# Attention with a gated convolution FFN on one core: low parts of the weights by TensorE and ScalarE, later q and k of the first batch transposed by TensorE, its V loaded for the whole batch, and order and banks from fixed tables

## The chip, the cores and the metric

The kernel runs on one core of a Trainium2 chip. The metric is the device time of one execution in microseconds (us). PE is TensorE, DVE VectorE, ACT ScalarE, POOL GpSimd; SP issues most DMAs. PEld is the loading of the stationary operand, which overlaps PE.

## The reference

```
scores = (q @ k.T) / 8, masked so that block i of 64 positions sees blocks j <= i
attn = softmax(scores);  x = attn @ v, heads put side by side     # [8, 576, 512]
h = relu(x @ w_in)                                                # [8, 576, 1024]
c[s] = w0*h[s-1] + w1*h[s] + w2*h[s+1]                            # per feature
out = (h * sigmoid(c)) @ w_out                                    # [8, 576, 512]
```

There are 8 batches, 8 heads of width 64, 576 positions, all in float32. The weights `w_in`, `conv_w` and `w_out` arrive as 64-bit floats and are turned into 32-bit ones on the chip ("decode").

## The kernel before, in words

**Arithmetic.** The two large products run in a short float format (float32r) that TensorE takes in one pass. To keep the precision, each operand is split into a high part, its float32r rounding, and a low part, the rest. A product is three matmuls: high by high, high by low, low by high. The parts are `wih`, `wil` for `w_in`, `woh`, `wol` for `w_out`, `x` (two halves) for the attention output and `gh`, `gl` for the gated hidden values. Scores and the product with V run in plain float32, in tiles of 64 rows by 32 columns.

**Attention.** Heads go in pairs, four pairs to a batch, 32 visits in all; the first batch is cut in two parts, so that its work can begin before the weights are there: part A takes the first 256 positions of four pairs, part B the other 320. A visit is: q and k transposed (by PE in part A, line 960; by DVE from a 32-by-32 layout otherwise, line 981, with q scaled by POOL on line 975), score matmuls (line 1010), row maxima on DVE (1023), exponentials with sums on ACT (1028), a merge of statistics (1044 to 1065), the scaling of the probabilities on POOL (1077), their transposition on DVE (1096), the product with V (1109), and the split of its result: ACT writes the high part (1123), DVE subtracts it from the PSUM bank and writes the low part (1126).

**FFN.** The batch is cut into two runs of positions ("halves"). Per half there are 8 chunks of 128 features. Twelve matmuls make a chunk (line 1156); ACT and DVE apply relu, convolution and gate (1170 to 1193), ACT writes `gh` (1193), POOL subtracts and writes `gl` (1196). The second layer takes, per 128 positions, three matmuls for each chunk (line 1222); ACT evicts and SP stores the result.

**Weights.** Sixteen chunks (eight of `w_in`, the first in two pieces, eight of `w_out`) are decoded by ACT (774), POOL (780) and DVE (785 to 808), POOL adding two parts on line 812 for four of them. ACT makes the high part (843). For twelve chunks the low part goes through PE: minus the high part (859) plus the decoded low term (862) is summed in a bank, and DVE adds the decoded main term to it (865). For four chunks POOL subtracts (846).

**Order.** Nothing is scheduled by hand. Every operation is recorded in a plan with a target time from a table of numbers (`TARGETS`). `Plan.order` then plays the engines forward with assumed durations, picks for each engine the ready operation with the least target, and hands out the eight PSUM banks as it goes. Where it expects PE to wait over 0.4 us, it puts in **fillers**: matmuls of a constant that nobody reads (line 1317), 512 columns each, 173 in all. Each engine executes its list in order.

Of the kernel before, what the change touches and what calls it, by code (L numbers as in the profile page):

```python
# [11 lines left out]
F32 = mybir.dt.float32  # L12
# [8 lines left out]
TARGETS = """  # L21
# [237 lines left out]

class Plan:  # L260

    DRAIN = (0.165, 0.08, 0.1, 0.025, 0.0)
    SIGNAL = (0.04, 0.035, 0.035, 0.08, 0.1)

    def __init__(self):
        self.ops = []
        self.tags = {}  # L270
        self.queue = {}

    def bank(self, slots, tag):
        b = Bank(slots, tag)
        q = self.queue.setdefault(tag, [])
        b.index = len(q)
        q.append(b)
# [36 lines left out]
    def order(self, targets, skip, fill, clock, pair):  # L314
# [13 lines left out]
        def use(o):  # L328
            t = o.start
            while t < o.end:  # L330
                w = int(t / step)
                u = min(o.end, (w + 1) * step)
                if u <= t:
                    u = t + 1e-6
# [1019 lines left out]
```

## Time and profile before

| | us |
|---|---|
| median of 3 runs | 749.32 (747.5 to 750.0) |
| the profiled execution | 750.95 |
| its span, first to last instruction | 749.2 |
| busy: PE, DVE, ACT, POOL | 687.9, 588.6, 528.2, 447.2 |

The profiled execution is 1.6 us above the median, and 1.75 us of it lie outside the span. PE's busy time counts fillers too, and records of neighbouring matmuls overlap, so that a busy PE need not be one at full rate.

### The profile page before, as it was taken

How to read it: one execution, taken by the hardware profiler on the slowest of the kernel's cores; microseconds unless marked ns; L12 is line 12 of the kernel's file. 1: busy time of each engine (PE TensorE's matmuls, PEld its weight loads, DVE VectorE, ACT ScalarE, POOL GpSimd, SP SyncE). 2: the span in 40 equal slices, each digit the busy share in tenths (PEclk: the TensorE clock that was granted, in tenths of full speed). 3: DMA queues.
4: the chain of work that ended last, by engine and by line, in shares of the span. 5: the costliest groups of instructions: out<-in, count | busy, mean ns of one | idle time of the engine just before them, and what ended most of it. 6: DMA issues, size and time to landing. Idle time of an engine off the chain costs nothing.

```text
span 749.2 us, 29948 instructions
## 1 busy us (share of the span) xinstructions
PE 687.9 (92%) x12112; PEld 562.6 (75%) x12112; DVE 588.6 (79%) x1422; ACT 528.2 (71%) x1987; POOL 447.2 (60%) x926
## 2 busy tenths in 40 slices
PE   8889887999989999898989989998989999998998
PEld 6567757767868787776868777786878687787986
DVE  5799996997888877898869868878868969876543
ACT  6667655787777757786877668767678768794554
POOL 1555884887467752767565746657546754776232
PEclk9999998999999999999999999999999999999999
DMA  8853655137423342335422352344304362122001
GB/s 197 179 108 74 125 124 110 32 71 150 82 44 85 67 106 34 77 70 90 83 64 46 54 130 50 57 93 81 74 12 90 79 126 35 44 52 63 1 29 43
DMA packets 238671, 58.59 MB, mean 78 GB/s; under 512 B 228652, under 2 KB 233028, under 8 KB 238532
## 3 DMA queue, kind: packets, MB, share of 16 engines
q1 hardware_dynamic: 237988, 56.55, 37.2%
q8 instruction: 95, 1.56, 0.9%
q14 instruction: 44, 0.36, 0.2%
q10 hardware_dynamic: 544, 0.13, 0.1%
HBM read 47.21 MB, written 9.44 MB: 76 GB/s over the span
## 4 chain that ended last, share of the span: by engine, by line
DVE 34%; ACT 18%; PE 17%; POOL 13%; issue 7%; DMA 5%; SPq 4%; DVEq 0%; POOLq 0%; ACTq 0%
ACT p L1028 11%; POOL p L1077 10%; DVE st L1023 7%; DVE ptw L1096 6%; PE banks L1222 6%; PE banks L1156 5%; DVE t L1177 4%; PE banks L1109 4%; DVE t L1181 4%; DVE t L1189 3%; PE banks L1010 2%; POOL gl L1196 2%; DMA kn<-in_k_dram 2%; ACT t L1173 2%; SPq L721 2%
## 5 line engine op out<-in xcount | busy, mean ns | idle before, releaser
L1077 POOL TENSOR_SCALAR p<-p,st 128x160 f32<-128x160 f32 (+8 forms) x576 | 247.7, 448 | 84.4 <-DVE st L1065 80.8
L1028 ACT ACTIVATE p<-banks,st 128x32 f32<-128x32 f32 (+8 forms) x576 | 220.4, 401 | 61.8 <-DVE st L1023 42.2
L1156 PE MATMUL banks<-x,wih 128*128 128x290 f32 (+3 forms) x1024 | 191.1, 302 | 4.2 <-DVE x L1126 1.7
L1196 POOL TENSOR_TENSOR gl<-t,gh 128x289 fp32r<-128x289 f32 (+3 forms) x128 | 108.2, 854 | 113.8 <-ACT gh L1193 99.3
L1156 PEld LDWEIGHTS banks<-x,wih 128*128 128x128 f32 x1024 | 156.1, 189 | 17.8 <-issue 4.2
L1096 DVE STREAM_TRANSPOSE ptw<-p 128x448 f32<-128x448 f32 (+8 forms) x272 | 131.6, 504 | 38.7 <-POOL p L1077 34.9
L1023 DVE TENSOR_REDUCE st<-banks 128x2 f32<-128x192 f32 (+8 forms) x288 | 127.3, 471 | 6.3 <-PE banks L1010 5.6
L1222 PE MATMUL banks<-woh,gl 128*128 128x512 f32 (+1 forms) x296 | 117.9, 398 | 7.7 <-POOL gl L1196 7.2
L1028 ACT ACTIVATION_READ_ACCUMULATOR p<-banks,st 128x1 f32 x576 | 122.8, 213 | 0.0
L1222 PE MATMUL banks<-woh,gh 128*128 128x512 f32 (+1 forms) x296 | 119.6, 404 | 1.1 <-ACT h L1170 0.6
L1222 PE MATMUL banks<-wol,gh 128*128 128x512 f32 (+1 forms) x296 | 115.7, 391 | 0.8 <-POOL wol L846 0.8
L1109 PE MATMUL banks<-ptw,vn 64*32 64x160 f32 (+8 forms) x4608 | 94.9, 300 | 22.1 <-issue 9.7
L1010 PE MATMUL banks<-kT,qT 64*32 64x96 f32 (+8 forms) x4320 | 100.7, 303 | 14.3 <-ACT p L1028 7.7
L1109 PEld LDWEIGHTS banks<-ptw,vn 64*32 64x32 f32 x4608 | 82.1, 107 | 39.9 <-issue 13.9
L1156 PE MATMUL banks<-x,wil 128*128 128x290 f32 (+3 forms) x512 | 108.8, 299 | 0.0
L1010 PEld LDWEIGHTS banks<-kT,qT 64*32 64x32 f32 x4320 | 66.7, 105 | 43.0 <-ACT p L1028 14.2
L1177 DVE SCALAR_TENSOR_TENSOR t<-h,cw,t 128x289 f32<-128x289 f32 (+3 forms) x128 | 70.4, 559 | 30.4 <-ACT t L1173 30.2
L1156 PEld LDWEIGHTS banks<-x,wil 128*128 128x128 f32 x512 | 82.8, 190 | 2.1 <-issue 1.3
L1186 ACT ACTIVATE t<-t 128x287 f32<-128x287 f32 (+3 forms) x128 | 56.4, 446 | 30.8 <-DVE t L1181 30.0
L1222 PEld LDWEIGHTS banks<-woh,gl 128*128 128x128 f32 x296 | 55.8, 189 | 28.7 <-POOL gl L1196 17.0
L1181 DVE SCALAR_TENSOR_TENSOR t<-h,cw,t 128x288 f32<-128x288 f32 (+3 forms) x128 | 73.0, 579 | 1.0
L1189 DVE SCALAR_TENSOR_TENSOR t<-t,h 128x287 f32<-128x287 f32 (+3 forms) x128 | 64.7, 511 | 10.0 <-ACT t L1186 9.6
(91 smaller groups left out, 801.6 us busy)
## 6 DMA issues: line engine op xcount, KB each, us to landing
vn<-in_v_dram SPq DMA_DIRECT2D x128, 144.0 KB, 3.7
out_dram<-stage SPq DMA_DIRECT2D x35, 256.0 KB, 2.6
kn<-in_k_dram SPq DMA_DIRECT2D x112, 72.0 KB, 2.7
qn<-in_q_dram SPq DMA_DIRECT2D x112, 72.0 KB, 2.5
x<-in_moe_w_out_dram SPq DMA_DIRECT2D x8, 512.0 KB, 4.5
gl<-in_moe_w_in_dram SPq DMA_DIRECT2D x4, 512.0 KB, 5.5
gh<-in_moe_w_in_dram SPq DMA_DIRECT2D x3, 512.0 KB, 5.3
vxa<-in_v_dram SPq DMA_DIRECT2D x16, 64.0 KB, 4.1
```

The lines of the kernel that those rows point to most:

```text
L1010: nc.tensor.matmul(both(sb)[32 * quad:32 * quad + 32, h, o:o + w].rearrange("p (u n) -> p u n", n=32), t["q"].ap[r, 64 * b + 32 * g:64 * b ...
L1023: nc.vector.tensor_reduce(out=st.ap[:, c:c + 2], in_=both(sb)[:, :, off:off + w], op=ALU.max, axis=AX.X, negate=True)
L1028: nc.scalar.activation(out=pt.ap[:, h, :], in_=both(sb)[:, h, off:off + w], func=AF.Exp, bias=st.ap[:, c:c + 1], accum_out=st.ap[:, n + c: ...
L1077: nc.gpsimd.tensor_scalar(out=pt.ap[:, h, :], in0=pt.ap[:, h, :], scalar1=st.ap[:, 5 * n + c:5 * n + c + 1], scalar2=0.0, op0=ALU.mult, op ...
L1096: nc.vector.transpose(pt.ap[:, :, b:b + rise * b + 1:rise, :], x.ap.rearrange("p h (u n) -> p h u n", n=32))
L1109: nc.tensor.matmul(both(vb)[o:o + 32, g, 32 * (lo - b0):32 * (b1 - b0)].rearrange("p (b n) -> p b n", n=32), vat(u, h)[r, 32 * y:32 * y + ...
L1156: nc.tensor.matmul(fb.ap[:, 0:n2], wt[:, c, fs], xs[c][xi].ap[:, x0:x0 + n2], start=(n + c - c0 == 0), stop=(n + c - c0 == 3 * NCC - 1))
L1177: nc.vector.scalar_tensor_tensor(out=t.ap[:, i0:no], in0=hb.ap[:, own + i0 - 1:own + no - 1], scalar=cw[:, f:f + 1], in1=t.ap[:, i0:no], o ...
L1181: nc.vector.scalar_tensor_tensor(out=t.ap[:, 0:i1], in0=hb.ap[:, own + 1:own + 1 + i1], scalar=cw[:, 2 * NFC + f:2 * NFC + f + 1], in1=t.a ...
L1189: nc.vector.scalar_tensor_tensor(out=t.ap[:, 0:no], in0=t.ap[:, 0:no], scalar=1.0, in1=hb.ap[:, own:own + no], op0=ALU.add, op1=ALU.mult)
L1196: nc.gpsimd.tensor_tensor(out=gbuf[1].ap[:, f, carry:carry + no], in0=t.ap[:, 0:no], in1=gbuf[0].ap[:, f, carry:carry + no], op=ALU.subtract)
L1222: nc.tensor.matmul(fb.ap[:, 0:cut], gbuf[a].ap[:, f, cs], w[:, f, ds], start=(f == 0 and n == 0), stop=(f == NFC - 1 and n == 2))
```

## The change

All 16 weight chunks now get their low part through PE and ACT. A third matmul brings the decoded main term into the same bank, in plain float32 against the identity, and ACT writes the sum out as the low part; the subtraction on DVE and that on POOL are gone, and so is the sum on POOL. The same is done for the low part of the attention output in the first batch: PE subtracts the high part in the bank, and ACT writes what is left. In part B, q and k come in rows of 64 values, PE transposes them (three matmuls for each of q and k of a pair) and ACT evicts them, scaling q. The values of V that part A needs are loaded by eight DMAs of 64 rows of all heads, instead of sixteen by head, and each product with V in part A waits for all eight. Two of the first weight loads are issued by ACT instead of SP. `Plan.order` is replaced by `Plan.follow`, which emits the operations in the order of a list, with the banks of a second list and 100 fillers at the places of a third.

```diff
@@ Plan
-    def order(self, targets, skip, fill, clock, pair):
...
+    def follow(self, order, banks, fills, work):
...
+        for x in order:
+            o = self.ops[x]
+            if x in fills:
+                z, k = fills[x]
...
+                work(z, k)()
...
+            o.fn()
@@ load_b (new; part B)
+                    nc.sync.dma_start(out=n.ap[0][0:r, c], in_=src[0, h0:h0 + 2, s:s + r, :].rearrange("h p d -> p h d"))
@@ load_first
-                        nc.sync.dma_start(out=vxa[64 * y:64 * y + 64, 2 * g + j],
-                                          in_=v[0, 2 * g + j, 0:Q1, :].rearrange("(u p) d -> p u d", p=64))
...
+                    nc.sync.dma_start(out=vxa[64 * y:64 * y + 64, :, u, :],
+                                      in_=v[0, :, 64 * u:64 * u + 64, :].rearrange("h p d -> p h d"))
@@ split
-        def fl():
-            nc.gpsimd.tensor_tensor(out=lo, in0=src(), in1=hi, op=ALU.subtract)
...
+        def mid():
+            nc.tensor.matmul(fb.ap[:, 0:n_], ident, scratch(None), start=False, stop=False)
...
         def fl2():
-            nc.vector.tensor_tensor(out=lo, in0=view(), in1=src(), op=ALU.add)
+            nc.scalar.activation(out=lo, in_=view(), func=AF.Copy)
@@ load_w_in
+            queue = nc.scalar if 0 < f + h < 2 else nc.sync
@@ later_t (new; part B)
+                    nc.tensor.matmul(tb.ap[:, c * P:c * P + r].bitcast(F32R), n.ap[1][0:r, c].rearrange("p j d -> p (j d)"), rident[0:r, 0:r],
+                                     start=(c == 0), stop=True, is_transpose=True, skip_group_check=True)
...
+            es.append(copy_op(False, S - Q1, lambda hi=hi: hi.ap[:, Q1:], lambda tb=tb: tb.ap[:, 0:S - Q1], at + 0.3, [o], [tb, hi], scale))
@@ stage_pv
+                nc.tensor.matmul(got()[:, g], nident, dst(0)[:, g], start=False, stop=True, skip_group_check=True)
...
+            nc.scalar.activation(out=dst(1), in_=got(), func=AF.Copy)
@@ end
-    for o in pl.order([int(x) for x in TARGETS.split()], SKIP, (work, psum, (NBANK0, NBANK, TB), 0.234, LEAST, SPARE), CLOCK, (NEAR, FAR, BIAS)):
-        o.fn()
+    pl.follow(ORDER, BANKS, FILLS, lambda z, k: work(psum[z], k))
```

What moves on the engines is seen in three places. In the lists below a row is a line of the kernel, an operation, what it writes and reads, and its size; the changed kernel's lines have other numbers.

**DVE, the first weight chunks.** `gh` is the staging buffer of a chunk here. Before:

```order
L801 TENSOR_SCALAR gh<-gh 128x256
L808 SCALAR_TENSOR_TENSOR wil<-gh 128x2x128
L865 TENSOR_TENSOR wil<-banks,gh 128x2x128
L785 TENSOR_SCALAR gh<-gh 128x512
L797 SCALAR_TENSOR_TENSOR gh<-gh 128x512
L801 TENSOR_SCALAR gh<-gh 128x512
L808 SCALAR_TENSOR_TENSOR wil<-gh 128x4x128
L1023 TENSOR_REDUCE st_277<-banks 128x2 x4
L865 TENSOR_TENSOR wil<-banks,gh 128x4x128
```

and now:

```order
L618 SCALAR_TENSOR_TENSOR gh<-gh 128x256
L622 TENSOR_SCALAR gh<-gh 128x256
L876 TENSOR_REDUCE st_267<-banks 128x2 x2
L632 SCALAR_TENSOR_TENSOR wil<-gh 128x2x128
L876 TENSOR_REDUCE st_267<-banks 128x2 x2
L904 TENSOR_TENSOR st_194<-st_194 128x8
L632 SCALAR_TENSOR_TENSOR wil<-gh 128x4x128
```

The final sum from the bank (L865) has left DVE in each chunk; the other steps stay.

**PE, ahead of the second product with V in part B.** `kX` and `kT` are transposed k, `ptw` the transposed probabilities, `vn` V, `rident` the constant of the fillers. Before:

```order
L1010 MATMUL banks<-kX,qT 32x160 x8
L1317 MATMUL banks<-rident 128x512 x41
L1109 MATMUL banks<-ptw,vn 32x160 x40
L1109 MATMUL banks<-ptw,vn 32x128 x8
L1109 MATMUL banks<-ptw,vn 32x96 x8
```

and now:

```order
L863 MATMUL banks<-kX,qT 32x288 x8
L863 MATMUL banks<-kX,qT 32x192 x8
L1020 MATMUL banks<-x,wih 128x256 x2
L814 MATMUL banks<-rident,kn_97 128x128 x2
L814 MATMUL banks<-rident,kn_97 128x64
L1020 MATMUL banks<-x,wil 128x256 x2
L1020 MATMUL banks<-x,wih 128x256 x2
L1181 MATMUL banks<-rident 128x512 x8
L962 MATMUL banks<-ptw,vn 32x160 x40
```

Of 41 fillers 8 are left; first-layer matmuls (L1020) and transposes (L814) stand between the scores and the product. Counted over the list up to the end of the fourth such product, fillers fall from 171 to 86, first-layer matmuls stay at 108, and second-layer ones go from 18 to 21.

**POOL, the fourth batch, chunks five and six of its first half.** The scalings of the probabilities (L1077, now L930) and the low parts `gl` (L1196, now L1060) share POOL's list. Before:

```order
L975 TENSOR_SCALAR qn<-qn 128x576
L1077 TENSOR_SCALAR p_6271<-p_6271,st_6226 128x64 x2
L1077 TENSOR_SCALAR p_6278<-p_6278,st_6226 128x128 x2
L1077 TENSOR_SCALAR p_6295<-p_6295,st_6226 128x32
L1077 TENSOR_SCALAR p_6285<-p_6285,st_6226 128x96
L1077 TENSOR_SCALAR p_71<-p_71,st_6226 128x160 x2
L1077 TENSOR_SCALAR p_6285<-p_6285,st_6226 128x96
L1196 TENSOR_TENSOR gl<-t,gh 128x287 x2
```

and now:

```order
L930 TENSOR_SCALAR p_71<-p_71,st_6148 128x160 x2
L930 TENSOR_SCALAR p_6191<-p_6191,st_6148 128x128 x2
L930 TENSOR_SCALAR p_6180<-p_6180,st_6148 128x32
L930 TENSOR_SCALAR p_6230<-p_6230,st_6148 128x64
L930 TENSOR_SCALAR p_6180<-p_6180,st_6148 128x32
L930 TENSOR_SCALAR p_6230<-p_6230,st_6148 128x64
L1060 TENSOR_TENSOR gl<-t,gh 128x287
L930 TENSOR_SCALAR p_6225<-p_6225,st_6148 128x96 x2
L505 TENSOR_SCALAR st_6337<-st_6337 32x16
L1060 TENSOR_TENSOR gl<-t,gh 128x287
```

Nine scalings stood ahead of the two low parts; now eight stand ahead of the first one. Over the 112 low parts behind the first batch, those with eight or more scalings right ahead of them go from 10 to 7.

## Rows read from the trace of the kernel before

**Rows 1.** The page, part 1: busy us of each engine (share of the span)

```profile
PE 687.9 (92%) x12112; PEld 562.6 (75%) x12112; DVE 588.6 (79%) x1422; ACT 528.2 (71%) x1987; POOL 447.2 (60%) x926
```

**Rows 2.** Stretches: busy of PE, PEld, DVE, ACT, POOL; clock, DMA share, GB/s

```profile
0.00:43.00 43.00, 35.69 (x560) 25.85 (x560) 29.09 (x86) 27.19 (x106) 17.88 (x47) 1.00 0.88 192
43.00:118.70 75.70, 67.09 (x1319) 51.25 (x1317) 72.95 (x173) 51.19 (x186) 51.36 (x92) 1.00 0.51 103
118.70:128.20 9.50, 6.34 (x35) 5.76 (x34) 4.39 (x11) 3.14 (x15) 5.68 (x11) 0.64 0.60 110
128.20:700.00 571.80, 532.93 (x9935) 439.57 (x9935) 458.21 (x1107) 418.72 (x1613) 356.67 (x758) 1.00 0.35 70
```

**Rows 3.** Waits of PE, 128.2 to 700 us: us, times, longest

```profile
PE banks L1222 <- POOL gl L1196: 7.2, 9, 1.5
```

**Rows 4.** POOL timeline, 366 to 382 us

```profile
375.28 3.98 POOL L1077 TENSOR_SCALAR p<-p,st 128x64 f32<-128x64 f32 x9 [0.73 <-DVE st L1065]
```

**Rows 5.** By stretch, of the fillers on line L1317 alone

```profile
0.00:43.00 43.00, 23.55 (x82) 15.90 (x82) 1.00 0.88 192
43.00:118.70 75.70, 23.02 (x91) 16.09 (x89) 1.00 0.51 103
```

**Rows 6.** PE timeline, 70 to 87 us: start, us, what, idle before

```profile
73.48 9.60 PE L1317 MATMUL banks<-rident 128*128 128x512 f32 x41
85.16 2.07 PE L1109 MATMUL banks<-ptw,vn 64*32 64x160 f32 x118 [2.07 <-ACT stage L774]
```

**Rows 7.** Chain of waits, first 45 us: start, us, what

```profile
36.45 6.56 DMA kn<-in_k_dram
```

**Rows 8.** PE timeline, 104 to 124 us

```profile
103.60 1.04 PE L1010 MATMUL banks<-kT,qT 64*32 64x288 f32 x32
...
116.55 2.18 PE L1109 MATMUL banks<-ptw,vn 64*32 64x160 f32 x131 [0.24 <-ACT st L1044]
121.89 0.35 PE L1109 MATMUL banks<-ptw,vn 64*32 64x32 f32 x13 [3.16 <-issue]
```

**Rows 9.** DVE groups, 0 to 128.2 us: count, busy us, mean ns

```profile
L1126 DVE TENSOR_TENSOR x<-banks,x 128x256 fp32r<-128x256 f32 (+1 forms) x8 | 3.5, 442 | 0.0
...
L865 DVE TENSOR_TENSOR wil<-banks,gh 128x512 fp32r<-128x512 f32 (+1 forms) x5 | 2.9, 574 | 0.9 <-PE banks L862 0.9
...
L865 DVE TENSOR_TENSOR wil<-banks,gl 128x512 fp32r<-128x512 f32 x4 | 2.7, 677 | 0.0
L865 DVE TENSOR_TENSOR wol<-banks,stage 128x512 fp32r<-128x512 f32 x4 | 2.7, 672 | 3.4 <-PE banks L862 3.4
```

**Rows 10.** DVE groups of the whole run, shapes apart

```profile
L981 DVE STREAM_TRANSPOSE qT<-qn 128x320 f32<-128x320 f32 x4 | 2.0, 504 | 0.7 <-POOL qn L975 0.7
...
L981 DVE STREAM_TRANSPOSE kT<-kn 128x320 f32<-128x320 f32 x2 | 1.0, 512 | 2.7 <-DMA kn<-in_k_dram 2.7
L981 DVE STREAM_TRANSPOSE kX<-kn 128x320 f32<-128x320 f32 x2 | 1.0, 508 | 0.0
```

**Rows 11.** Line L865 by stretch

```profile
43.00:118.70 75.70, 3.35 (x5) 1.00 0.51 103
```

**Rows 12.** Line L1126 by stretch

```profile
43.00:118.70 75.70, 2.26 (x5) 1.00 0.51 103
```

**Rows 13.** ACT groups, 0 to 128 us, shapes apart

```profile
L843 ACT ACTIVATE wih<-gl 128x512 fp32r<-128x512 f32 x4 | 2.6, 639 | 0.4 <-DVE gl L797 0.4
...
L1123 ACT ACTIVATE x<-banks 128x320 fp32r<-128x320 f32 x4 | 1.7, 434 | 2.3 <-PE banks L1109 2.3
```

**Rows 14.** POOL groups, 0 to 128 us, shapes apart

```profile
L812 POOL TENSOR_TENSOR stage<-stage,x 128x512 f32<-128x512 f32 x3 | 4.1, 1360 | 0.7 <-POOL st L696 0.7
...
L846 POOL TENSOR_TENSOR wol<-stage,woh 128x512 fp32r<-128x512 f32 x3 | 3.9, 1293 | 0.9 <-ACT woh L843 0.9
```

**Rows 15.** PE timeline, 22 to 25 us

```profile
22.93 0.60 PE L1109 MATMUL banks<-pta,vxa 64*32 64x128 f32 x26 [0.19 <-DVE pta L1096]
```

**Rows 16.** SP timeline, 26 to 45 us

```profile
27.73 1.26 SPq L762 DMA_DIRECT2D vxa<-in_v_dram  x2
```

More of the change, by code (lines that the diff above doesn't have):

```diff
@@ L1 @@
-import heapq
-from collections import deque
 from functools import partial
@@ new lines, in follow @@
+    def follow(self, order, banks, fills, work):
+        order = [int(x) for x in order.split()]
+        place = {x: i for i, x in enumerate(order)}
+        assert len(place) == len(order) == len(self.ops)
+        for o in self.ops:
+            assert all(place[d.seq] < place[o.seq] for d in o.deps)
+        every = [b for q in self.queue.values() for b in q]
+        banks = "".join(banks.split())
+        assert len(banks) == len(every)
+        for b, z in zip(every, banks):
+            b.slot, b.left = int(z), len(b.uses)
+        tenant = {}
+        fills = {int(x): (int(z), int(k)) for x, z, k in (f.split(":") for f in fills.split())}
+        for x in order:
+            o = self.ops[x]
+            if x in fills:
+                z, k = fills[x]
+                assert tenant.get(z) is None
+                work(z, k)()
@@ L504, in order @@
             for b in o.banks:
+                assert tenant.get(b.slot) in (None, b)
+                tenant[b.slot] = b
                 b.left -= 1
-                b.rel = max(b.rel, o.end + o.lat + self.DRAIN[e] + self.SIGNAL[PE] if e != PE else o.end)
                 if not b.left:
-                    tenant[b.slot], freed[b.slot], past[b.slot] = None, b.rel, b.uses
-                    gone[b.tag] += 1
-            free[e] = o.end
-            if o.port:
-                port = o.end
-            done.append(o)
@@ L514, in order @@
-            for c in o.outs:
-                c.left -= 1
-                lat = self.DRAIN[e] + (self.SIGNAL[c.eng] if c.eng != e else 0.0) if (e != PE or c.eng != PE) else 0.0
-                rtime[c.seq] = max(rtime[c.seq], o.end + o.lat + lat)
-                if e != PE:
-                    wtime[c.seq] = early[c.seq] = rtime[c.seq]
-                if c.left == 0:
-                    if c.eng == PE:
-                        open_.append(c)
-                    else:
-                        heapq.heappush(future[c.eng], (rtime[c.seq], c.target, c.seq, c))
@@ L525, in order @@
-        done.sort(key=lambda o: o.start)
-        return done
+                    tenant[b.slot] = None
+            o.fn()
 @with_exitstack
@@ L639 @@
     firstq, firstp = Bin([]), Bin([])
+    qkn = []
+    for x in "qk":
+        at = place(x + "n", S)
+        qkn.append([fixed(f"{x}n{y}", s, d, at) for y, (s, d) in enumerate((([P, S // 32, 32], F32), ([P, 3, 2, D], F32), ([P, 3, 2, D], F32R)))])
     def held(tag, t, cap, before=None):
@@ L724, in load_qk, with load_b, go @@
             res.append((n, ops))
+        return res
+    def load_b(p, at):
+        h0, res = 2 * p, []
+        for z, src in enumerate((q, k)):
+            n = held(("qn", "kn")[z], [qkn[z][1:]], 1)
+            def go(src=src, n=n):
+                for c in range(3):
+                    r = min(P, S - Q1 - c * P)
+                    s = Q1 + c * P
+                    nc.sync.dma_start(out=n.ap[0][0:r, c], in_=src[0, h0:h0 + 2, s:s + r, :].rearrange("h p d -> p h d"))
+            res.append((n, [pl.op(SP, 1.7, go, at + 0.1 * z, bufs=[n], xfer=c_dma(2 * (S - Q1) * D * 4, 256))]))
         return res
@@ L811, in s7, with s8 @@
             def s7(j=j, words=words):
-                nc.gpsimd.tensor_tensor(out=scratch(j), in0=scratch(j), in1=words(1).bitcast(F32), op=ALU.add)
+                ap = [words(0).bitcast(F32), words(1).bitcast(F32)]
+                if low:
+                    ap = [low(j)] + [x.rearrange("p (c f) -> p c f", f=P) for x in ap]
+                else:
+                    ap = ap[:1] + ap
+                nc.gpsimd.tensor_tensor(out=ap[0], in0=ap[1], in1=ap[2], op=ALU.mult)
+            def s8(j=j, words=words):
+                nc.gpsimd.tensor_tensor(out=scratch(j), in0=scratch(j), in1=words(0).bitcast(F32), op=ALU.add)
             o4 = pl.op(DVE, c_dve(n) + 0.05, s4, at, deps=[o3], bufs=bufs, port=True)
             o = pl.op(DVE, c_dve(n, True), s5, at, deps=[o4], bufs=bufs, port=True)
-            o = pl.op(DVE, c_dve(n) + 0.06, s6, at, deps=[o], bufs=bufs, port=True)
-            fin.append(pl.op(POOL, c_pool(n, True), s7, at, deps=[o], bufs=bufs) if not low else (o4, o))
+            if low and not alt:
+                fin.append((o4, pl.op(DVE, c_dve(n) + 0.06, s6b, at, deps=[o], bufs=bufs, port=True)))
+                continue
+            o6 = pl.op(ACT, c_act(n, False) + 0.04, s6, at, deps=deps, bufs=bufs)
+            o = pl.op(POOL, c_pool(n, True), s7, at, deps=[o, o6], bufs=bufs)
+            fin.append(pl.op(POOL, c_pool(n, True), s8, at, deps=[o], bufs=bufs) if not low else (o4, o))
         return fin
@@ L829, in split @@
         at += JW[f]
-        ld = pl.op(SP, 0.4 if f < NFC else 1.0, go, (at - WLEAD if f >= NFC else WL0 + WLS * f) + JD[f], deps=deps, bufs=bufs, xfer=1.9 / share if f < NFC else 2.1)
-        whole = f not in WPE
+        ld = pl.op(SP if go.queue is nc.sync else ACT, 0.4 if f < NFC else 1.0, go, (at - WLEAD if f >= NFC else WL0 + WLS * f) + JD[f], deps=deps, bufs=bufs, xfer=1.9 / share if f < NFC else 2.1)
         nc_ = c_ // len(parts)
@@ L835, in low @@
             return lo[:, nc_ * j:nc_ * j + nc_, :]
-        o = decode(parts, scratch, [ld], bufs, at, None if whole else low, f in S2P)
+        o = decode(parts, scratch, [ld], bufs, at, low, f in S2P, f in LOWA)
         def src():
@@ L843, in fh @@
             nc.scalar.activation(out=hi, in_=src(), func=AF.Copy)
-        def fl():
-            nc.gpsimd.tensor_tensor(out=lo, in0=src(), in1=hi, op=ALU.subtract)
-        if whole:
-            o1 = pl.op(ACT, c_act(512), fh, at + 1, deps=o, bufs=bufs)
-            wdone[f] = pl.op(POOL, c_pool(512, True), fl, at + 1, deps=[o1], bufs=bufs)
-            return pl.ops[first:]
-        fb = bank("f")
+        fb = bank("w")
         def view():
@@ L965, in first_t, with later_t, tr @@
             es.append(copy_op(False, Q1, lambda hi=hi: hi.ap[:, 0:Q1], lambda tb=tb: tb.ap[:, 0:Q1], at + 0.3, [o], [tb, hi], scale))
+        return t, es
+    def later_t(nat, at):
+        t = {"q": two([P, S], F32, "qT"), "k": firstk.pop(0)}
+        es = []
+        for (n, lds), nm, scale in zip(nat, "qk", (SCALE, 1.0)):
+            tb, hi = bank("q"), t[nm]
+            def tr(n=n, tb=tb):
+                for c in range(3):
+                    r = min(P, S - Q1 - c * P)
+                    nc.tensor.matmul(tb.ap[:, c * P:c * P + r].bitcast(F32R), n.ap[1][0:r, c].rearrange("p j d -> p (j d)"), rident[0:r, 0:r],
+                                     start=(c == 0), stop=True, is_transpose=True, skip_group_check=True)
+            o = pl.op(PE, run(tr_(), tr_(), tr_(P, 64)), tr, at, deps=lds, bufs=[n, tb], area=0.7)
+            es.append(copy_op(False, S - Q1, lambda hi=hi: hi.ap[:, Q1:], lambda tb=tb: tb.ap[:, 0:S - Q1], at + 0.3, [o], [tb, hi], scale))
         return t, es
@@ L1126, in evl, with back, evp @@
             nc.vector.tensor_tensor(out=dst(1), in0=got(), in1=dst(0), op=ALU.subtract)
+        def back():
+            for g in range(2):
+                nc.tensor.matmul(got()[:, g], nident, dst(0)[:, g], start=False, stop=True, skip_group_check=True)
+        def evp():
+            nc.scalar.activation(out=dst(1), in_=got(), func=AF.Copy)
         e = pl.op(ACT, c_act(2 * w), evh, at + 3.0, deps=[o], bufs=vb + [xx[0]])
+        if part:
+            e = pl.op(PE, run(*[mm_(w)] * 2), back, at + 3.2, deps=[e], bufs=vb + [xx[0]])
+            es = [pl.op(ACT, c_act(2 * w), evp, at + 3.3, deps=[e], bufs=vb + [xx[1]])]
+            return ready(es)
         es = [pl.op(DVE, c_dve(2 * w), evl, at + 3.3, deps=[e], bufs=vb + [xx[0], xx[1]])]
```

248 lines of the change are left out of this document (38 added, 210 removed), and 350 rows, old and new, of tables (ORDER, TARGETS).

## The prediction, made before the changed kernel ran

> **What bounds the kernel now.** I read the page first, then tables by stretch, then timelines where PE waits, and last the chain of waits. PE is the busiest engine [rows 1], but the time falls apart into stretches of different kind [rows 2].
>
> Behind 128 us PE is the bound: 532.9 us busy of 571.8, so 38.9 us idle, in many short waits. One kind is a wait for POOL's low part `gl`, 7.2 us in 9 waits [rows 3]; at the longest of them POOL has just done nine scalings of probabilities in 3.98 us [rows 4], which its list put ahead of the low part.
>
> The first 118.7 us look different. PE is shown busy for 35.7 and 67.1 us, but 23.6 and 23.0 us of that are fillers [rows 2, 5]: PE does its own work in about 56 of 118.7 us, and is waiting in the rest. The clearest place is ahead of the second product with V in part B, where 41 fillers last 9.60 us and are followed by 2.07 us of nothing [rows 6]. From 43 to 118.7 us DVE is busy 72.95 of 75.7 us, 96%, while ACT and POOL have 51 each [rows 2]. So DVE bounds this stretch. From 0 to 43 us DVE has 29.1 us and the DMA engines are at 0.88 of their time [rows 2]; the chain of waits ends this stretch with 6.56 us for the k of part B [rows 7]. So loads bound it.
>
> Between the two comes a hole: at 118.7 us PE stops within a product with V and goes on 3.16 us later, with no releaser shown [rows 8]. In the 9.5 us from there the granted clock averages 0.64 [rows 2], that is, part of them at 1.2 instead of 2.4 GHz.
>
> **The change part by part.**
>
> *DVE.* The final sum of the low part goes, 2.9 + 2.7 + 2.7 = 8.3 us for 13 pieces, and the low part of the attention output, 3.5 us for 8 [rows 9]. So do eight transposes of 320 columns, 2.0 + 1.0 + 1.0 = 4.0 us [rows 10]. That is 15.8 us. In the DVE-bound stretch lie 3.35 us of the first [rows 11], 2.26 us of the second [rows 12] and, I take it, 3 of the 4 us of transposes: 8.6 us. DVE then has 64.3 us there, and at the same 96% the stretch lasts 66.8 us: a gain of up to 8.9 us.
>
> *ACT.* It takes over 16 chunks' low parts, eight of the attention output, and eight evictions of 320 columns. A copy from PSUM of 320 columns takes 0.434 us and one of 512 within SBUF 0.639 us [rows 13]; I take 0.6 for 512, 0.43 for the others: 16 x 0.6 + 16 x 0.43 = 16.5 us, some 11 of them in the stretch. ACT then has 62 of 67 us there, nearly as full as DVE. What is queued behind these copies on ACT are the exponentials, and PE's products with V wait for those in the end. So the full 8.9 us won't come.
>
> *POOL.* Sums of 1.36 us and subtractions of 1.29 us leave for four chunks [rows 14], 10.6 us in all. POOL has 24 us to spare in this stretch [rows 2], so I count nothing for it.
>
> *PE.* It loses 73 fillers. 41 took 9.60 us [rows 6], so 0.234 each, 17.1 us. It gains 16 plain float32 matmuls of 512 columns. The trace has none of that size. Below: the 0.234 us of a filler, which has the same columns in the short format. Above: a score group, two pieces of 288 and 192 columns in the plain format, takes 1.04 us [rows 8], which makes 1.11 us for 512. I take the upper end, since the format is the same: 17.8 us (3.7 at the lower). The Trainium skill, page FP8 and Floating Point Precision, section TensorE Precision Notes, says that true float32 takes four passes through the array; by that each costs four fillers, an estimate of 0.94 us, and the sixteen 15.0. Four chunks more take the two short matmuls, 8 x 0.234 = 1.9 us; 24 transposes and 16 subtractions of up to 160 columns come to 40 x 0.07 = 2.8 us at the filler's rate per column. Together 22.5 us in, 17.1 out: +5.4 us of PE work, -8.7 at the lower end. PE's list up to the end of part B shows the same sum: 85 fillers fewer, 20 us, against some 21 us of new work. By this count alone the stretch stays as it is; by DVE's load it loses 8.9 us. Fillers stand in waits, though, and a wait that ends earlier takes its filler along: ahead of the second product in part B only 8 of 41 are left, with first-layer matmuls in their place. I take **-5 us** for 43 to 118.7, between 0 and -8.9.
>
> *Loads.* The same bytes, in fewer and longer pieces: rows of 64 values for q and k of part B, eight DMAs for V, two weight loads by ACT's idle queue. The first stretch is bound by bytes that stay, so **-1 us**, between +3 (the rival on V, below) and -2.
>
> *The hole.* The 3.16 us and the slow clock behind it (9.5 us at 0.64, so at most 3.4 us lost) hang on where the lists and DMAs stand; the new lists move all of that. It may be gone or turn up elsewhere: half, **-3 us**, between 0 and -6.6.
>
> *Behind 128 us* the work is the same and only the order new. Low parts with eight or more scalings ahead go from 10 to 7; three tenths of 7.2 us [rows 3] are **-2 us**, between +5 (the new list may make waits of its own, as many as two thirds of these) and -7.
>
> Sum: -1 - 5 - 3 - 2 = -11 us. The profiled execution took 750.95 us, its span of 749.2 and 1.75 around it, 1.6 above the median of 749.32. So 739.95 in its terms and **738 us** in those of the median.
>
> **The rivals.**
>
> *PE takes the relief back (slower).* If the waits that the fillers stood in stay, because PE's own new matmuls (each third one needs the decoded word, the high part and a bank) now stand in front of scores and products in PE's list, the stretch grows by PE's 5.4 us and nothing is gained: 749.3 + 5.4 = 755 us. It decides from the point where PE has under 5 us of wait left in 43 to 118.7; before it has 8.6 idle and 23.0 in fillers. For it: three engines near full. Against: the 32 us of slack.
>
> *ACT takes DVE's place.* If ACT's 11 us lie in front of the exponentials, the stretch keeps its length, and -1 - 3 - 2 are left: 743 to 745 us.
>
> *The clock falls more often.* In the trace the clock fell once early, after the 3.16 us of nothing [rows 8], and a fall cost at most 3.4 us. With half the fillers gone in the first part, two or three more falls give 738 + 7 to 10: 745 to 748 us, no change. For it: PE does waiting without filler where the list expects none. Against: the list keeps fillers in its long waits, and the engine is fed more of its own work. The Trainium skill, page TensorE: Matmul & The Clock Gate, section What's actually happening, speaks for this rival: throttled is the default, and activity releases it. The trace agrees in the hole; for fewer fillers no run here shows it yet.
>
> *V by whole batch.* The first product with V starts at 22.93 us [rows 15], when the last V loads have not been issued, which happens at 27.73 [rows 16]. Now it waits for all of them. That costs up to 5 us at this product, and since the others of part A follow behind it, up to 3 on the path; then 741.
>
> *All of it comes.* -2 - 8.9 - 6.6 - 5: 727 us.
>
> **How the numbers follow.** The forecast case, 730 to 746, has 0.57 (V's rival lies in it); everything, below 730, 0.13; ACT 0.08; the clock 0.08; slower 0.14. A measurement of this kernel can tell about 0.3%, 2.2 us, from no change. Faster by more: 0.57 + 0.13 and most of ACT's and a little of the clock's, 0.76; the same: 0.10; slower: 0.14. The range 725 to 752 leaves out some 0.07 below and 0.11 above.
>
> **What would show it.** In the profile after: part B's fourth product with V ends near 112 instead of 118.7 us; DVE between 43 us and there is at 63 to 66 us and ACT at 60 or more; about 23 us of fillers in all instead of 47; the third matmul of a chunk starts its successor 0.9 to 1.1 us later; PE's waits for `gl` are at 5 us. The forecast is wrong if that product ends at 117 or later (PE or ACT took it back), if the granted clock shows several falls before 130 us, or if PE's idle time behind part B, 38.9 us before, moves by more than 8 us: then the new order, which I priced at 2 us, is the main thing.

## The result, and the profile after

| | before | after |
|---|---|---|
| median of 4 runs on one chip | 749.66 us (747.5 to 751.8) | 706.7 us (704.8 to 707.4) |
| the profiled execution, its span | 750.95, 749.2 | 706.31, 704.5 |

The ratio is 0.9423, with a 95% interval from 0.939 to 0.9456: 43 us faster, where 11 were forecast, and below the range that began at 725.

The first part of the page after, which answers [rows 1]:

```profile
PE 673.6 (96%) x12121; PEld 559.8 (79%) x12121; DVE 579.2 (82%) x1392; ACT 538.7 (76%) x2021; POOL 447.0 (63%) x915
```

The fourth product with V in part B, around whose stop the forecast cut the time, ends at 122.2 us before (behind the hole of [rows 8]) and at 107.8 us now. The stretches of before, cut there, with the columns of [rows 2]:

```profile
43.00:122.20 79.20, 67.43 (x1333) 51.49 (x1331) 74.01 (x176) 52.78 (x196) 53.18 (x97) 0.99 0.52 103
122.20:749.20 627.00, 584.76 (x10228) 485.28 (x10222) 485.54 (x1160) 448.21 (x1685) 376.17 (x783) 0.99 0.33 67
```

and those of the changed kernel:

```profile
0.00:43.00 43.00, 39.09 (x649) 28.38 (x656) 26.66 (x86) 32.19 (x127) 21.94 (x53) 1.00 0.77 186
43.00:107.80 64.80, 61.26 (x1179) 44.61 (x1181) 59.83 (x142) 56.71 (x188) 39.15 (x79) 1.00 0.57 125
107.80:704.50 596.70, 573.30 (x10319) 486.78 (x10307) 492.73 (x1166) 449.78 (x1708) 385.88 (x785) 1.00 0.36 71
```

So 14.4 us came from the part up to there, the head, and 30.3 from the part behind it, 627.0 to 596.7, in which the two kernels do the same work. PE's idle time there fell from 627.00 - 584.76 = 42.2 to 596.70 - 573.30 = 23.4 us, and its busy time by 11.5 us; the two make up the 30.3. Some 3 us of this belong to the slow clock that followed the hole (before, the granted clock is 0.50 from 123 to 126 us and 0.73 from there to 130, an estimate of 1.5 + 1.1 us lost). The end of the head is known to some 4 us only: in t_early below, whose lists and banks are those of the changed kernel up to there, it stands at 111.5 us. The fillers in the first and second stretch, which answer [rows 5], are down from 46.6 to 25 us:

```profile
0.00:43.00 43.00, 20.06 (x69) 13.32 (x69) 1.00 0.77 186
43.00:107.80 64.80, 4.90 (x17) 2.96 (x17) 1.00 0.57 125
```

In PE's timeline the second product of part B, which answers [rows 6], stands behind 8 fillers and no wait, and the fourth, which answers [rows 8], runs without a hole:

```profile
72.64 2.11 PE L1181 MATMUL banks<-rident 128*128 128x512 f32 x8
74.82 2.30 PE L962 MATMUL banks<-ptw,vn 64*32 64x160 f32 x144
...
105.54 2.27 PE L962 MATMUL banks<-ptw,vn 64*32 64x160 f32 x142
107.61 0.33 PE L863 MATMUL banks<-kT,qT 64*32 64x160 f32 x2
107.63 0.21 PE L962 MATMUL banks<-ptw,vn 64*32 64x32 f32 x2
```

Behind the head the waits changed on every engine. Before, 122.2 to 749.2 us, one line from each of four engines' tables (us, times, longest):

```profile
PE banks L1010 <- ACT p L1028: 6.9, 9, 1.4
DVE ptw L1096 <- POOL p L1077: 33.4, 60, 2.0
ACT p L1028 <- DVE st L1023: 40.2, 34, 4.9
POOL gl L1196 <- ACT gh L1193: 93.4, 44, 10.8
```

After, 107.8 to 704.5 us, the same waits, and PE's for `gl`, which was 7.2 us in [rows 3]:

```profile
PE banks L863 <- ACT p L881: 3.0, 3, 1.4
PE banks L1086 <- POOL gl L1060: 0.3, 1, 0.3
DVE ptw L949 <- POOL p L930: 8.7, 18, 1.1
ACT p L881 <- DVE st L876: 26.6, 26, 3.2
POOL gl L1060 <- ACT gh L1057: 64.3, 38, 8.9
```

POOL's wait fell by the most, 29.1 us; of the three longer ones DVE's fell by the largest share: 60 transposes of probabilities waited 33.4 us for POOL's scaling, now 18 wait 8.7. Not every wait fell: those of PE with no releaser shown ("issue"), for scores and products with V, went from 8.5 to 13.1 us, and DVE's for `x` from ACT from 18.6 to 24.7. The wait that the forecast counted is a small one among them.

### The profile page after: what moved, and what is told of

Read it like the earlier page. It is cut to its first block, busy times and chain, and to the rows that moved or that the text cites. A ratio compares the mean times of both kernels' runs of the same rounds, so it can differ in the third digit from the quotient of the medians.

```text
span 704.5 us, 29942 instructions
## 1 busy us (share of the span) xinstructions
PE 673.6 (96%) x12121; PEld 559.8 (79%) x12121; DVE 579.2 (82%) x1392; ACT 538.7 (76%) x2021; POOL 447.0 (63%) x915
## 5 line engine op out<-in xcount | busy, mean ns | idle before, releaser
L930 POOL TENSOR_SCALAR p<-p,st 128x160 f32<-128x160 f32 (+8 forms) x576 | 260.2, 472 | 69.5 <-DVE st L918 59.9
L881 ACT ACTIVATE p<-banks,st 128x160 f32<-128x160 f32 (+8 forms) x576 | 220.3, 400 | 39.9 <-DVE st L876 27.1
L1020 PE MATMUL banks<-x,wih 128*128 128x288 f32 (+3 forms) x1024 | 190.3, 301 | 0.8 <-ACT p L881 0.5
L1020 PEld LDWEIGHTS banks<-x,wih 128*128 128x128 f32 x1024 | 156.5, 188 | 15.1 <-issue 6.0
L1060 POOL TENSOR_TENSOR gl<-t,gh 128x289 fp32r<-128x289 f32 (+3 forms) x128 | 109.5, 861 | 84.8 <-ACT gh L1057 64.3
L876 DVE TENSOR_REDUCE st<-banks 128x2 f32<-128x256 f32 (+8 forms) x288 | 125.4, 472 | 17.5 <-PE banks L863 16.4
L949 DVE STREAM_TRANSPOSE ptw<-p 128x576 f32<-128x576 f32 (+8 forms) x272 | 127.0, 496 | 10.3 <-POOL p L930 8.7
L1086 PE MATMUL banks<-woh,gl 128*128 128x512 f32 (+1 forms) x296 | 115.4, 390 | 0.3 <-POOL gl L1060 0.3
L1020 PE MATMUL banks<-x,wil 128*128 128x290 f32 (+3 forms) x512 | 106.7, 299 | 0.0
L1020 PEld LDWEIGHTS banks<-x,wil 128*128 128x128 f32 x512 | 82.3, 188 | 5.0 <-issue 2.2
L1045 DVE SCALAR_TENSOR_TENSOR t<-h,cw,t 128x288 f32<-128x288 f32 (+3 forms) x128 | 77.4, 611 | 2.1
L505 POOL TENSOR_SCALAR st<-st 32x16 f32<-32x16 f32 (+2 forms) x136 | 32.1, 236 | 69.1 <-ACT p L881 40.3
L1037 ACT ACTIVATE t<-h,cw 128x289 f32<-128x289 f32 (+3 forms) x128 | 68.1, 537 | 8.0 <-POOL gl L1060 4.9
L1053 DVE SCALAR_TENSOR_TENSOR t<-t,h 128x289 f32<-128x289 f32 (+3 forms) x128 | 66.1, 524 | 8.0 <-ACT t L1050 6.9
```

The lines of the kernel that those rows point to most:

```text
L876: nc.vector.tensor_reduce(out=st.ap[:, c:c + 2], in_=both(sb)[:, :, off:off + w], op=ALU.max, axis=AX.X, negate=True)
L881: nc.scalar.activation(out=pt.ap[:, h, :], in_=both(sb)[:, h, off:off + w], func=AF.Exp, bias=st.ap[:, c:c + 1], accum_out=st.ap[:, n + c: ...
L930: nc.gpsimd.tensor_scalar(out=pt.ap[:, h, :], in0=pt.ap[:, h, :], scalar1=st.ap[:, 5 * n + c:5 * n + c + 1], scalar2=0.0, op0=ALU.mult, op ...
L949: nc.vector.transpose(pt.ap[:, :, b:b + rise * b + 1:rise, :], x.ap.rearrange("p h (u n) -> p h u n", n=32))
L1020: nc.tensor.matmul(fb.ap[:, 0:n2], wt[:, c, fs], xs[c][xi].ap[:, x0:x0 + n2], start=(n + c - c0 == 0), stop=(n + c - c0 == 3 * NCC - 1))
L1037: nc.scalar.activation(out=t.ap[:, 0:no], in_=hb.ap[:, own:own + no], func=AF.Copy, scale=cw[:, NFC + f:NFC + f + 1])
```

## The experiments

Theory O says that the new order of the lists is worth the 30 us behind the head by itself. Its rivals: the banks (B), the head, which lets the rest flow (H), and the clock with its fillers (F). All kernels were timed beside the kernel before, which stood at 748.2 to 749.7 us; intervals are 95% of the ratio to it.

### Order against banks and head

**c_banks**, the new lists with banks taken anew:

```diff
-BANKS, FILLS: the tables of the changed kernel
+BANKS, FILLS: the bank that has been free longest; the order yields where there is none
```

> The changed kernel with its own order of operations, but with the PSUM banks taken anew by a plain rule (the bank that has been free longest); where a bank is not free at an operation's place in the list, the operation moves back a little (17 places of TensorE's list change, 10 of VectorE's, 6 of ScalarE's). Theory O (the order of the lists is what gained): the time stays at 706.7 us, within 4 us. Rival B (the table of banks gained, by fewer waits for a bank's reader): it goes back by a good part of the 43 us, to 720 us or more.

729.98 us, 0.9747 (0.9727 to 0.9766): 23 us lost. It mixed two things, three late operations and banks reused soon (22 of 463 within 1 us of TensorE work, 9 in the changed kernel's table), so nothing follows yet.

**a_oldbehind** and **b_newbehind**, two grafts with the same bank rule:

```diff
 a_oldbehind: arithmetic and operations 0 to 789 as in the changed kernel
-ORDER: operations 790 to 5276 in the new order
+ORDER: operations 790 to 5276 in the order of the kernel before
 b_newbehind: arithmetic and operations 0 to 763 as in the kernel before
-order of operations 764 to 5250 by Plan.order
+order of operations 764 to 5250 by Plan.follow and the new list
```

> The changed kernel's arithmetic and its order for the weights and the first batch (operations 0 to 789), but everything behind (the first batch's second feed-forward half and all later visits, operations 790 to 5276, the same operations in both kernels) in the order of the kernel before; banks by the longest-free rule. The stretch behind the first batch went from 627.0 to 596.7 us, the part up to there from 122.2 to 107.8. Theory O (the new order behind is worth its 30 us by itself): 706.7 + 30.3 = 737 us, of 730 to 742. Rival H (the head carries it: less work and an earlier start, and what follows runs as well in either order): 707 to 712 us.

> The opposite graft: the kernel before with its own arithmetic and its own order for the weights and the first batch (operations 0 to 763), and the changed kernel's order for everything behind; lists and banks fixed in tables. Theory O: 749.7 - 30.3 = 719 us, of 714 to 726. Rival H (the head carries it): 745 to 750 us. If both grafts give less than their halves, to 737 or more each, the order needs its own head, and neither alone is the cause.

746.24 us, 0.9971 (0.9952 to 0.999), and 751.04 us, 1.0044 (1.0023 to 1.0064). Neither half seemed to carry the gain. But both had the soon reused banks of the first control (28 and 15 within 1 us), so the next three took them out. For a_oldbehind itself this was not done, so what the new head gives with the old order behind it stays open.

**c_exact** and **d_banks**, each kernel's own lists, unmoved, with banks searched for late reuse; **b_exact**, the second graft with such banks and without late operations:

```diff
-BANKS, FILLS of c_banks, of the kernel before, of b_newbehind
+BANKS, FILLS: searched, so that a bank's next use stands far behind its last; no operation moves
```

> The changed kernel with its list of the order kept exactly (no operation moves on any engine), and a new table of banks that was searched for long distances between a bank's last use and its next: of 463 reuses 17 come within 2 us of TensorE work (43 in its own table), 5 within 1 us (9). In the first control (729.98 us) three of TensorE's operations had also moved back by 2.7 to 3.5 us, so it mixed two things. Theory O (the lists of the order are what counts): 706.7 us, within 4. Rival B (its own table of banks holds the gain): 715 us or more. If waits for banks still cost something, 700 to 704 us.

> The kernel before in every operation, in its own order on every engine, with banks by the same search in place of the planner's: of its reuses 7 come within 2 us of TensorE work (52 in its own), 2 within 1 us (10). Theory O: banks are no part of it, 748 us, within 4. Rival B (waits for banks stall TensorE in the kernel before, and fixed tables may cure this): 735 to 742 us.

> The kernel before with its own arithmetic and order for the weights and the first batch, and the changed kernel's order behind, now without the three late operations that the first graft of this kind (751.04 us) shared with the first control; banks by search, as in the other run of this call. Behind the first batch that graft took 620.6 us, the first control 618.9, the changed kernel 596.7, the kernel before 627.0. Theory O (the exact order behind is worth about 30 us by itself): 122 to 126 us for the head and 597 to 602 behind, 720 to 730 us. Rival H (it needs its own head): 740 us or more.

c_exact 710.6 us, 0.9474 (0.9436 to 0.9512); d_banks 749.63, 0.9995 (0.9975 to 1.0014); b_exact 726.24, 0.9691 (0.9667 to 0.9715). Better banks give the old order nothing, and other banks leave the new one within 4 us; the new order on the old head gives 23.5 us. b_exact's stretches, head to 123.1 us and behind, and d_banks' stretch behind its head:

```profile
43.00:123.10 80.10, 69.33 (x1250) 51.22 (x1248) 71.42 (x167) 48.12 (x168) 50.40 (x91) 0.96 0.49 97
123.10:726.20 603.10, 576.28 (x10318) 487.94 (x10314) 496.65 (x1171) 450.90 (x1714) 388.41 (x789) 1.00 0.36 71
```

```profile
120.90:747.40 626.50, 580.88 (x10222) 485.03 (x10222) 486.50 (x1160) 448.31 (x1685) 377.33 (x783) 1.00 0.33 67
```

The head of b_exact is that of before, and 603.1 us follow instead of 627.0, with 26.8 us of PE idle instead of 42.2. DVE's wait for the scaling is down there too, behind the old head:

```profile
DVE ptw L920 <- POOL p L901: 8.9, 19, 1.1
```

So O holds for 24 of the 30 us, and H falls. d_banks shows also that the clock isn't it: at a granted clock of 1.00, the old order still takes 626.5 us behind its head.

**s_late** and **c_three**, which ask what lost 23 us in c_banks. s_late moves one score operation; c_three has the three late operations of c_banks, with searched banks:

```diff
 TensorE's list in s_late, by number
-4122 4158 3913 3924 3889 3878 3890 3914
+4122 3913 3924 3889 3878 3890 4158 3914
```

> As the run c_exact of this call but for one score operation (number 4158, the first scores of a block pair at about 510 us), which stands five places (2.65 us of TensorE work) later in TensorE's list; its VectorE readers move back by one place each, and no other operation moves on its engine. Theory D (the list is tight: in-order queues hand one late operation on, so that it costs more than its own shift): 3 to 8 us more than c_exact. Rival L (TensorE works on something else in between, so that a late operation costs nothing): c_exact's time, within 2 us.

> The lists of the first control (729.98 us: the changed kernel's, but a weighted sum at about 380 us and the first scores at about 390 and 510 us stand 2.7 to 3.5 us later in TensorE's list, with their readers), with the searched banks of c_exact (710.6 us). Theory E (three late operations add up, and gaps of TensorE bring the slow clock): 725 us or more. Rival B (the first control's banks, 22 of which were reused within 1 us of TensorE work, lost most of it): 709 to 716 us.

711.23 us, 0.9483 (0.9456 to 0.951), and 712.18, 0.9503 (0.9479 to 0.9528). Late scores cost next to nothing; D and E fall. The same lists took 730 us with the other banks: 18 us were lost by banks alone. So banks can ruin an order, but what the two kernels had was good enough in both.

### What in the order

**t_late** and **t_early** move DVE's transposes of probabilities, in DVE's list alone. A place in t_early:

```diff
 L1045 SCALAR_TENSOR_TENSOR t<-h,cw,t 128x288
+L949 STREAM_TRANSPOSE ptw<-p_74 128x2x8x32
 L834 STREAM_TRANSPOSE qT<-qn_92 128x576
 L876 TENSOR_REDUCE st_6997<-banks 128x2
-L949 STREAM_TRANSPOSE ptw<-p_74 128x2x8x32
```

> The kernel before (with the table of banks of d_banks, 749.63 us), with one edit to one engine's list: behind the first batch, 194 of the 252 VectorE transposes of normalized probabilities (ptw from p) stand later, so that the median TensorE work between the POOL normalization and the transpose that reads it grows from 0.70 to 1.6 us (1.70 in the changed kernel). No other engine's list changes. Behind part B VectorE waited 33.4 us in 60 places for these normalizations in the kernel before and 8.7 us in 18 in the changed one. Theory T (these waits, by which everything behind in VectorE's queue comes late, are the main part of what the new order saved): those waits fall to 10 to 15 us, and the time to 730 to 740 us. Rival M (the new order saves by many small distances on all engines, of which this is one): 743 to 750 us.

> The opposite edit: the changed kernel (706.7 us) with its own banks, 244 of the same 252 transposes earlier in VectorE's list, so that the median distance behind the normalization falls from 1.70 to 0.30 us (0.70 in the kernel before); all else as it was. Theory T: VectorE's waits for POOL's p rise from 8.7 to 30 us or more, and the time to 720 us or more. Rival M: 707 to 714 us.

t_early 729.05 us, 0.9729 (0.969 to 0.9768): 22 us slower than the changed kernel. Of that, 17.9 us of the profiled execution lie behind the head, where the one edited list is (614.6 against 596.7 us); the head, which the edit leaves alone, ended 3.7 us later. t_late 758.1, 1.0135 (1.0098 to 1.0172): 8.5 us slower than d_banks, whose lists it shares but for the edit. In t_early, the stretch and the wait in question:

```profile
111.50:726.10 614.60, 577.83 (x10315) 488.23 (x10301) 498.10 (x1166) 450.17 (x1708) 381.56 (x785) 1.00 0.35 69
DVE ptw L961 <- POOL p L942: 20.3, 43, 1.4
```

In d_banks behind its head, and then the same waits in t_late (124.2 to 760.2 us):

```profile
DVE ptw L920 <- POOL p L901: 32.6, 59, 2.1
DVE st L875 <- POOL st L520: 16.9, 9, 4.8
DVE st L847 <- PE banks L834: 6.0, 10, 1.1
PE banks L933 <- DVE ptw L920: 4.8, 8, 1.6
PE banks L834 <- ACT p L852: 9.3, 12, 1.7
```

```profile
DVE ptw L920 <- POOL p L901: 21.1, 42, 2.1
DVE st L875 <- POOL st L520: 24.0, 14, 4.9
DVE st L847 <- PE banks L834: 12.4, 16, 2.1
PE banks L933 <- DVE ptw L920: 3.4, 5, 1.1
PE banks L834 <- ACT p L852: 9.6, 13, 2.0
```

In t_late DVE waits 11.5 us less for the scaling, though not as little as theory T expected. But DVE's waits for POOL's statistics and for the scores, which now come earlier in its list, grew by 7.1 and 6.4 us, and PE's waits for transposes and exponentials hardly changed. So the wait was handed on within DVE's list, the time behind the head rose from 626.5 to 636.0 us, and T in its simple form falls. What in t_late makes these 9.5 us isn't shown; part of it is PE's slow clock (0.97 from 300 to 400 us, 1.00 in d_banks). In t_early the time is what T said, but DVE's wait grew by 11.6 us, to 20.3 and not to 30; M said too little.

**p_slack**, the old planner with the new constants:

```diff
-    DRAIN = (0.165, 0.08, 0.1, 0.025, 0.0)
+    DRAIN = (0.265, 0.18, 0.2, 0.125, 0.0)
+    PAD = (0.0, 0.03, 0.025, 0.04, 0.0)
```

> The kernel before in all but two constants of its planner, which take the changed kernel's values: the delay from an operation's end to its reader grows by 0.1 us on every engine, and VectorE, ScalarE and POOL operations are planned 0.03, 0.025 and 0.04 us longer. Its own planner then makes a new order out of the same due times. Theory S (the new order is better because it was planned with longer delays, so that readers stand further behind): a large part of the 30 us, 720 to 735 us. Rival R (the gain is in the particular lists, which another search found): no gain, 745 to 760 us.

803.76 us, 1.0752 (1.0728 to 1.0776). Planning with longer delays makes no better list out of these due times. S falls, at least with them; R's range, 745 to 760 us, was too low too.

### The fillers and the head

**f_nofill**, no fillers at all:

```diff
-FILLS: 19 places, 100 matmuls
+FILLS: empty
```

> The changed kernel without its 100 filler matmuls (28.8 us, of which 20.1 in the first 43 us and 3.8 behind 112 us); the operations themselves are the same, in the same order. Theory F (the fillers hold the clock, which stayed at 1.0 from 4.2 us on): the granted clock falls to 0.5 more than once, 3 us or more lost at each fall, 712 to 725 us. Rival N (they only fill waits): 704 to 708 us, within 2 us of the changed kernel, with the half-rate stretch at the start longer than 4.2 us.

704.24 us, 0.9408 (0.9385 to 0.9431), no different from the changed kernel. N holds for the time, though not for the clock at the start. The plain float32 matmul against the identity, the third of a chunk, early and late in PE's timeline (start, us):

```profile
21.09 1.91 PE L687 MATMUL banks<-gh,ident 128*128 128x512 f32 x2
...
37.58 1.07 PE L687 MATMUL banks<-gl,ident 128*128 128x512 f32 x2
```

The first ran at little more than half the rate of the second, so the clock was still at the lower of its two levels, 1.2 GHz, at 21 us; only the rates tell this, for the clock column shows 1.00 from 0 to 43 us. The head ended at 111.9 us, about where it ends in t_early with all its fillers (111.5), and behind it this kernel took 591.3 us instead of 596.7. The Trainium skill, page TensorE: Matmul & The Clock Gate, section What's actually happening, holds that throttled is the default and activity releases the clock; the early row agrees. No price of it shows in the time here.

**u_low**, **u_evl**, **u_tr**, **u_v** undo one edit each in the new order; **u_all** and **u_all2** all four. In u_all a load buffer that pairs share is overwritten before it is read, so that it does not compute the same thing; u_all2 has buffers that pairs use in turn:

```diff
 u_low
-            nc.tensor.matmul(fb.ap[:, 0:n_], ident, scratch(None), start=False, stop=False)
-            nc.scalar.activation(out=lo, in_=view(), func=AF.Copy)
+            nc.vector.tensor_tensor(out=lo, in0=view(), in1=src(), op=ALU.add)
 u_evl
-            nc.scalar.activation(out=dst(1), in_=got(), func=AF.Copy)
+            nc.vector.tensor_tensor(out=dst(1), in0=got(), in1=dst(0), op=ALU.subtract)
 u_tr
+                nc.vector.transpose(hi.ap[:, Q1:].rearrange("p (t n) -> p t n", n=32), w)
 u_v
+                        nc.sync.dma_start(out=vxa[64 * y:64 * y + 64, 2 * g + j],
```

> The changed kernel (706.7 us), where only the low parts of the weights are added by VectorE again at the place of the ScalarE copy; the plain float32 matmul between is left out. Theory A (the arithmetic shortened the head): this is the largest piece of VectorE work, 20 additions of 0.57 to 0.68 us, some 11 us of VectorE in the first 107 us; 4 to 10 us slower, 711 to 717 us. Rival K (VectorE has room in the new order): within 2 us of 706.7.

> The changed kernel, where only the low parts of the first batch's attention are subtracted by VectorE again (8 subtractions of 0.44 us, 3.5 us in all, and no TensorE matmul nor second ScalarE copy). Theory A: 1 to 3.5 us slower, 708 to 710 us. Rival K: within 2 us of 706.7, or faster, since a chain of two engines replaces one of three.

> The changed kernel, where only the later rows of the first batch's q and k are scaled by POOL and transposed by VectorE again (8 transposes of about 0.5 us, 4 scalings of POOL), at the places of the changed kernel's ScalarE copies and TensorE transposes, with load buffers that two pairs share in turn. Theory A: 2 to 6 us slower, 709 to 713 us, since VectorE's transposes must also wait for loads that arrive in smaller pieces. Rival K: within 2 us of 706.7.

> The changed kernel, where only V of the first batch is loaded by pairs of heads again (eight loads as before, in the same places of the queue, each of one pair's half, so that a weighted sum waits for two of the loads and not for all). Theory V (V's loads are the missing part): 714 to 718 us. Rival T (together the edits overfill VectorE, each alone finds room): 705 to 709 us; the first weighted sum then ends before 31.1 us.

> The changed kernel with all of its arithmetic undone in place: the weights' low parts are added by VectorE again (no plain float32 matmul, no ScalarE copy), the first batch's attention low parts are subtracted by VectorE, its later q and k are scaled by POOL and transposed by VectorE, V is loaded by pairs of heads; each at the place in the new order where the changed kernel does its own, the lists and banks kept. Theory O (all is in the order, the head's too): 707 to 712 us. Rival A (the new arithmetic is what made the first 107.8 us shorter by 14.4 us, the order behind gave the rest): 718 to 726 us, all of it lost by the end of the fourth weighted sum of part B.

> As the earlier run u_all (721.36 us; there one shared load buffer was overwritten by the third pair's q before the second pair's was transposed, so that this part of its output was another's), but with buffers that pairs use in turn: all arithmetic of the first batch and V's loads undone in place. Theory A: still 716 to 722 us, with the fourth weighted sum of part B at 116 to 122 us. Rival W (the earlier loss was mostly the one stall behind a late load and the slow clock after it): 707 to 713 us.

One by one: 707.11 us (0.9423 to 0.947), 706.78 (0.9415 to 0.9458), 708.87 (0.9439 to 0.9482), 708.18 (0.9416 to 0.9476), none apart from the changed kernel's interval. All four: 721.36 (0.9601 to 0.9668) in u_all and, without the shared buffer, 719.51 (0.9562 to 0.9635). The head of u_low, to 110.5 us, and u_all2's stretches, head to 116.5 us:

```profile
43.00:110.50 67.50, 54.93 (x1142) 42.40 (x1148) 65.43 (x152) 50.34 (x174) 36.96 (x77) 0.97 0.51 118
```

```profile
43.00:116.50 73.50, 57.39 (x1198) 43.76 (x1202) 70.91 (x166) 50.09 (x174) 42.41 (x86) 0.88 0.54 109
116.50:713.10 596.60, 573.12 (x10313) 486.67 (x10301) 495.95 (x1169) 450.11 (x1708) 383.88 (x786) 1.00 0.36 71
```

DVE is back at 70.91 of 73.5 us, 96%, as in [rows 2], and the head is longer by 8.7 us; behind it nothing is lost. That is the profiled execution, 714.92 us, the fastest of four; where the others (to 721.23) lost more isn't shown. One by one the edits cost 4.2 us in sum, together 12.8, so that A and K are each right for a part: the arithmetic and V's loads are worth 12.8 of the 43 us, 8.7 of it seen in the head (some of it slow clock, 0.88 here). Why they cost more together stays open. DVE's load alone doesn't tell: u_low has DVE at 97% of its head and is no slower. Theory W, one stall, falls.

## Why the prediction was wrong

The failed step is "*Behind 128 us* the work is the same and only the order new", priced at -2 us, at most -7. The runs put -24 (b_exact, old head) to -30.3 us there, some 3 us of it the clock behind the hole. The price came from one wait on one engine, PE's for `gl`, and from one count in POOL's list. That wait did go, 7.2 to 0.3 us, but the other named waits of PE and most of the long ones behind them on DVE, ACT and POOL shrank with it, and PE's idle time, the one figure that adds up PE's waits, stood in the second paragraph: 38.9 us. A new order of all lists can reach all of it, so it, and not one wait, was the size to think of. It isn't a strict bound either: 18.8 of the 30.3 us came off idle time and 11.5 off busy time. The last sentence of the prediction named this case, by PE's idle time moving by more than 8 us; b_exact confirms it.

The other steps:

- **The DVE-bound stretch**, -5: the direction was right, the term too small. DVE has 59.83 us of 64.8 there now, 92%, and in u_all2 the 96% come back with the old arithmetic, but u_low's 97% at no cost leave it unproven that DVE's load set the length. The head as a whole gave 14.4 us (10.7, if it ends as in t_early) against 9 (-1, -5, -3); the runs don't part loads (-1) from the rest. ACT has 56.7 us and didn't take DVE's place.
- **PE's new matmuls**, 1.11 us each: mis-sized, on the high side. The start of one and of the score matmul right behind it:

```profile
59.62 1.02 PE L689 MATMUL banks<-stage,ident 128*128 128x512 f32 x2
60.57 0.50 PE L863 MATMUL banks<-kT,qT 64*32 64x160 f32 x16
```

0.95 us apart; another comes to 0.86 (last section). PE's work without fillers did grow in the head, from 56.6 to 75.4 us by the stretches above, but in the place of fillers and waits, so the rival of 755 us didn't come. The Trainium skill, page FP8 and Floating Point Precision, section TensorE Precision Notes, speaks of four passes for true float32; the estimate of 0.94 us that the prediction worked out from it agrees with this row.
- **The hole and the clock**, -3: the hole is gone, 3.16 us in the head and some 3 behind it, so this term came nearly whole; the granted clock is shown at 1.00 in all three stretches. More falls of the clock, the rival of 745 us, didn't come with fewer fillers.
- **V by whole batch**, a rival of +3: the first product with V does start at 29.81 us instead of 22.93, but the head is shorter all the same, and u_v, which keeps the list's place for the product, found no cost.

What stays open is how the 24 to 30 us divide among the distances of the new lists. Only one kind was tried, and only its loss (18 us behind the head) is shown, not its gain. Of the 11.5 us of PE's busy time, 7.6 are there against d_banks too, at the same clock and for much the same matmuls; the tables don't say why.

## What to carry to other kernels

Where every list is fixed by a table, price a new table from the whole idle time of the bounding engine in its stretch (42.2 us here, of which 18.8 went), not from the one wait that can be seen to change. Distances between a writer and its reader on another engine are a property of all lists at once: moving one engine's instructions towards their readers or writers, in both runs that tried it, cost time and brought other waits. And test an order with its banks: a graft with carelessly reused banks (b_newbehind) took 25 us more than b_exact and gave a wrong verdict.

## What the runs showed of the hardware

- Two kernels with the same lists differed by 18 us when 22 instead of 5 of 463 banks were reused within 1 us of TensorE work, by the planner's durations (c_banks, c_three). Part of it came as slow clock: the stretch around c_banks' longest pause of PE (3.24 us), and the same stretch of c_three:

```profile
494.00:545.00 51.00, 45.88 (x754) 37.73 (x751) 39.52 (x90) 33.90 (x127) 33.70 (x65) 0.93 0.31 59
494.00:545.00 51.00, 47.90 (x859) 40.05 (x858) 39.98 (x89) 37.21 (x142) 31.73 (x59) 1.00 0.32 64
```

- A plain float32 matmul of 512 columns is recorded as two instructions, and where a short-format one follows, that one's row starts halfway, so that the cost shows two rows on. In the changed kernel:

```profile
20.52 1.02 PE L689 MATMUL banks<-gh,ident 128*128 128x512 f32 x2
20.98 0.79 PE L692 MATMUL banks<-wil,rident 128*128 128x512 f32 x1
21.61 2.47 PE L1181 MATMUL banks<-rident 128*128 128x512 f32 x10
```

  From 20.52 to 21.61 us are 1.09 us; less a filler's 0.234 for the short one, 0.86 us are left for the plain one.
